# Two constants of a build-time planner: the pace of attention beside an MLP, and how late TensorE counts a cast of v

## The chip, the cores and the metric

The kernel runs on one core of a Trainium2 chip. The metric is device time in microseconds (us) of one execution. Thirteen runs of the kernel before gave a median of 348.4 us, from 345.13 to 350.83.

## What is computed

Attention with a causal mask, 8 batches and 8 heads, 576 query tokens, head size 64. Sixteen "beacon" keys and values stand ahead of the 576 own ones and are never masked. The attention output, as 4608 tokens by 512, goes through a two-layer MLP with a squared ReLU:

```python
k_all = np.concatenate([beacon_k, k], axis=2)
v_all = np.concatenate([beacon_v, v], axis=2)
scores = scale * np.matmul(q, k_all.transpose(0, 1, 3, 2))
scores = np.where(causal, -1e9, scores)
a = softmax(scores)
x = np.matmul(a, v_all)        # then (B, S, H*D) -> (4608, 512)
h = x @ w_in                   # 512 -> 2048
g = np.maximum(h, 0.0) ** 2
out = g @ w_out                # 2048 -> 512
```

## The kernel before

**Attention** works on pairs of heads: 4 pairs in each of 8 batches, pairs 0 to 31, so pair 16 is the first of batch 4, pair 20 of batch 5, pair 24 of batch 6, pair 28 of batch 7. From batch 1 on a pair has two groups of score matmuls (L622, into two PSUM strips each; the first group 4 matmuls, the second 8), four exponentials on ScalarE (L637), two causal minima on VectorE (L648, L651; "the mask"), and two attention-times-V groups of 15 matmuls, one per head (L674, into a PSUM tile `ps`). VectorE divides by the row sums (L692, L694) into `xn`. Groups of batch 0 are cut smaller.

**The MLP** works on chunks of 512 tokens, 9 chunks over 4608 tokens. A batch has 576 tokens, so chunk j crosses batches: chunk 3 needs batches 2 and 3, chunk 4 needs 3 and 4, chunk 5 needs 4 and 5. A chunk has 16 first-layer groups of 4 matmuls (L805; chunk 4 crosses the end of a ring buffer and has 8 of 256 columns, the first four of which need batch 3 alone; chunk 0 is cut into 240 and 272 columns), a ReLU each on ScalarE or VectorE (L821, L823), squares on VectorE (L830), and 16 second-layer groups of 4 matmuls (L840; "w_out groups"). ScalarE or VectorE copies the result to `osb` and SyncE stores it (L868).

**The MLP's input** is xT, the transpose of `xn`. For batches 0 to 2 TensorE transposes (L742); from batch 3 on SyncE issues five DMA transposes per batch (L725), of 112, 128, 128, 128 and 80 tokens. Chunk 3 needs the first three of batch 3, chunk 4 the first three of batch 4, chunk 5 the first two of batch 5.

**Loads.** q, k and v come in float32 pieces of up to 128 tokens (q0 to q4, k0 to k4, v0 to v4 of a batch) into eight staging buffers `stg` (L365; the beacons L364), on GpSimd's queue for batches 0 and 1, on SyncE's from batch 2 on. GpSimd casts each piece to bf16 (L320); the buffer is then free for another load. From batch 2 on SyncE issues two DMA transposes per batch (L398), qT after the five q casts and kT after the five k casts; scores need both. So SyncE's one queue, in program order, holds loads, the transposes of q and k, the transposes to xT, and the stores.

**What sets the order.** Nothing of the order is decided on the chip. `Order.run` (L69 to L190) plays the program through at build time: each operation has engines, a duration, a priority, dependencies and buffers, and each engine takes the ready operation of lowest priority number. The order in which it starts operations becomes the program's order on each engine; the chip keeps that order on each engine and waits on semaphores where data is late. Three things bear on the change:

- An operation that uses another's result is ready some time after it (L98 to L103). Users on TensorE have an event of their own, put off by the producer's `late`:

```python
heapq.heappush(events, (seen, seq, "done", op))
seq += 1
heapq.heappush(events, (seen + op.late, seq, "done_pe", op))
```

- Casts of v from batch 1 on have `late` 2.0 (L392). Their users on TensorE are the attention-times-V groups (L682 to L685).
- Attention is metered by MLP progress (L584, L591 to L594). `progress` sums the durations of the MLP groups started so far; pair p is held until it has reached

```python
return o.progress >= mlp_chunk_us * (LEAD + PACE * (p - HP))
```

with `mlp_chunk_us` 27.7, `LEAD` -0.4, `PACE` 0.255 and HP 4. MLP groups have priority numbers of 100,000 and more (L781), attention of some thousands at most, so attention runs as soon as its gate and its data allow, and the MLP fills the rest.

Of the kernel before, what the change touches and what calls it, by code (L numbers as in the profile page):

```python
# [45 lines left out]
class Order:  # L46
# [16 lines left out]
    def add(self, *a, **kw):  # L63
        op = Op(*a, **kw)
        op.need = [d for d in op.need if d is not None]
        self.ops.append(op)
        return op
# [126 lines left out]
def kernel(  # L194
# [116 lines left out]
    def rows_of(c):  # L311
        return 128 if c < NT - 1 else LAST
# [3 lines left out]
    def copy_on(e, dst, src):  # L316
        if e == "ACT":
            nc.scalar.copy(dst, src)  # L318
        else:
            eng[e].tensor_copy(dst, src)  # L320
# [12 lines left out]
    def t_start(t):  # L333
        return max(0, 128 * t - Nb)
# [14 lines left out]
    def add_load(b, x, c, prio, behind=[], sync=[]):  # L349
        t, beacon = src[x]  # L350
        lo = Nb if (c == 0 and beacon is not None) else 0
        if x == "q":
            t0, rows = 128 * c, min(128, S - 128 * c)
        else:
            t0, rows = t_start(c), rows_of(c)

        soft = b <= 1
        queue = nc.gpsimd if soft else nc.sync

        def emit_load(e):  # L360
            st = stg[ld.held[2]]
            insts = []
            if lo:
                insts.append(queue.dma_start(out=st[0:Nb], in_=beacon[b].transpose([1, 0, 2])))  # L364
            insts.append(queue.dma_start(out=st[lo:rows],  # L365
                                         in_=t[b, :, t0:t0 + rows - lo, :].transpose([1, 0, 2])))
            return insts

        ld = add(f"ld{b}{x}{c}", "POOL" if soft else "SP", 1.3 if lo else 0.65, emit_load,
                 prio=prio, take=("stg", "stg"), dma=(1.15 if b < NPE else 1.25) * rows / 128, behind=load_chain[-1:] + behind, sync=sync)  # L370
        load_chain.append(ld)

        def emit_cast(e):
            st = stg[ld.held[2]]
            if x == "v":
                copy_on(e, vb[b % 2][0:rows, c, :, 0:D], st[0:rows])
            else:
                dst = (qb if x == "q" else kb)[b % 2][0:rows, :, c, :]
                copy_on(e, dst, st[0:rows].rearrange("p (g u) d -> p g (u d)", u=2))

        deps = [ld]
        if x == "v" and b >= 2:
            deps += [o for p in range(HP * (b - 2), HP * (b - 1)) for o in av_ops[p]]
        if x != "v":
            if b < NPE + 2:
                deps += [zero_ops[b]]
            else:
                deps += trans[b - 2, x]
        engs = ("POOL", "DVE") if b == 0 and c <= 1 else ("POOL",)
        cast[b, x, c] = add(f"cast{b}{x}{c}", engs, {"DVE": 0.6, "POOL": 0.65}, emit_cast,  # L390
                            prio=prio if b else prio - 220.0, deps=deps, give=ld,
                            late=2.0 if x == "v" and b > 0 else 0.0)  # L392

    def add_trans(b, x, prio):
        srcb, dst = (qb, qT) if x == "q" else (kb, kT)
# [185 lines left out]
        return SPLIT if p < NSPLIT else WHOLE  # L581

    mlp_chunk_us = 27.7
    LEAD, PACE = -0.4, 0.255  # L584
    norm_ops = {}

    def add_pair(b, pr):
# [291 lines left out]
    late = []  # L879
    for b in range(B):  # L880
# [8 lines left out]
        for n, (x, c) in enumerate(([] if b < NPE else nat) + [("v", c) for c in range(NT)]):  # L889
            behind, sync = [], []  # L890
            if x == "v" and b == 0:
                pass
            elif x == "v" and b == 1 and c == 0:
                behind = [strided[1, 0, HP - 1, "q"]]
            elif b == 2 and n == 0:
                sync = [w_ops["out", 3]]
            elif b >= NPE and x == "v" and c == 0:
                for y in "qk":
                    add_trans(b, y, lp - 5.0)
                behind = trans[b, "q"] + trans[b, "k"]  # L900
            add_load(b, x, c, lp + 0.1 * n, behind, sync)
            if x == "v":
                v_loads[b].append(load_chain[-1])
# [13 lines left out]
        if b >= 1:  # L917
            for j in late:
                add_chunk(j)
            late = []  # L920
# [48 lines left out]
```

The softmax here doesn't subtract the row's maximum and nothing guards it: scores larger than these inputs give would overflow.

## Time and profile before

| what | value |
|---|---|
| median of 13 runs | 348.4 us |
| the profiled execution | 349.01 us |
| its span, first to last instruction of the program | 347.3 us |
| mean granted TensorE clock | 0.995 |
| TensorE's last matmul ends | 343.4 us |
| DMA traffic | 51.70 MB, mean 149 GB/s |

Times inside the span count from its first instruction; the 1.7 us between span and time lie around it. PE is TensorE's matmul stream, PEld its weight loads, DVE VectorE, ACT ScalarE, POOL GpSimd, SPq the queue of SyncE. "Busy" sums the time in which an instruction ran. In a wait line, the engine and line that waited come first, then what ended the wait, then total us, times and the longest. In a timeline line, start, length, engine, line, operation and operands; square brackets hold idle time ahead of it and what ended it. A DMA's length in SyncE's timeline is the time to issue it, not to land it; the view of a tile and the chain of waits give the landing. The trace misses 41 of 2957 matmul records, so a group of four can show as three.

### The profile page before, as it was taken

The numbers are of one execution on the slowest core, as the hardware profiler recorded it, in microseconds if no ns is written. First come the engines' busy times: TensorE is split into PE (matmuls) and PEld (weight loads), VectorE is DVE, ScalarE is ACT, GpSimd is POOL, SyncE is SP. The second block draws the span as 40 slices with busy tenths as digits, with TensorE's granted clock in tenths as the row PEclk, the third lists the DMA queues.
The fourth block names the chain that finished last, engine by engine and source line by source line (L and its number), as shares of the span: only waits on it lengthen the run. The fifth ranks groups of instructions, "written<-read, shape, count | busy, mean of one in ns | idle before, by whom it ended". The sixth has DMA issues, their size and how long they took to land.

```text
span 347.3 us, 7286 instructions
## 1 busy us (share of the span) xinstructions
PE 334.2 (96%) x2916; PEld 179.8 (52%) x2957; DVE 169.9 (49%) x366; ACT 193.8 (56%) x293; POOL 93.7 (27%) x144
## 2 busy tenths in 40 slices
PE   8999899999999999999989997999999999999995
PEld 7577665444554544445458743444444454444442
DVE  6796874258536852565336633473256412301300
ACT  3887664377657644775447644475467616615611
POOL 9674904325316425120523155012000000000000
PEclk9999999999999999999999999899999999999999
DMA  8999979999999999689999999891520032011002
GB/s 144 211 206 206 205 127 213 226 242 210 190 230 232 205 198 210 148 182 143 208 141 234 217 189 170 201 213 24 106 85 2 0 105 86 2 60 61 0 26 97
DMA packets 143664, 51.70 MB, mean 149 GB/s; under 512 B 130670, under 2 KB 138382, under 8 KB 143630
## 3 DMA queue, kind: packets, MB, share of 16 engines
q1 hardware_dynamic: 135231, 42.25, 61.8%
q0 software_dynamic: 7904, 8.69, 14.8%
q8 instruction: 23, 0.38, 0.5%
q10 hardware_dynamic: 495, 0.30, 0.3%
q14 instruction: 11, 0.09, 0.1%
HBM read 37.22 MB, written 9.44 MB: 134 GB/s over the span
## 4 chain that ended last, share of the span: by engine, by line
PE 75%; DMA 12%; POOL 5%; SPq 4%; issue 1%; DVE 1%; ACT 1%; POOLq 0%; ACTq 0%
PE ps L805 32%; PE ps L840 30%; PE strip L622 6%; PE ps L674 6%; DMA stg<-in_v_dram 4%; DMA qk_area<-in_q_dram 4%; DMA xT<-xn 3%; POOL qk_area L443 2%; DMA stg<-in_k_dram 1%; SPq L398 1%; SPq L725 1%; POOL vb L320 1%; SPq L365 1%; POOL stg L365 1%; PE ps L742 1%
## 5 line engine op out<-in xcount | busy, mean ns | idle before, releaser
L805 PE MATMUL ps<-xT,w_in 128*128 128x512 bf16 (+3 forms) x689 | 134.2, 342 | 4.2 <-DMA xT<-xn 3.5
L840 PE MATMUL ps<-w_out,g 128*128 128x512 bf16 x550 | 130.5, 379 | 1.8 <-issue 0.8
L637 ACT ACTIVATE pt<-strip 128x832 bf16<-128x832 f32 (+4 forms) x128 | 103.8, 863 | 28.6 <-PE strip L622 28.3
L805 PEld LDWEIGHTS <-w_in 128*128 128x128 bf16 x704 | 65.3, 98 | 60.6 <-issue 7.0
L821 ACT ACTIVATE g<-ps 128x512 bf16<-128x512 f32 (+2 forms) x123 | 68.4, 556 | 46.7 <-PE ps L805 45.8
L840 PEld LDWEIGHTS <-g 128*128 128x128 bf16 x576 | 52.5, 98 | 61.8 <-issue 4.4
L830 DVE TENSOR_TENSOR g<-g 128x1024 bf16<-128x1024 bf16 (+2 forms) x80 | 51.4, 647 | 58.6 <-ACT g L821 57.2
L320 POOL CAST qk_area<-stg 128x512 bf16<-128x512 f32 (+2 forms) x60 | 41.1, 692 | 59.8 <-DMA stg<-in_k_dram 39.2
L318 ACT COPY osb<-ps 128x512 f32<-128x512 f32 x32 | 18.8, 586 | 66.2 <-PE ps L840 45.6
L320 POOL CAST vb<-stg 128x512 bf16<-128x512 f32 (+1 forms) x39 | 26.5, 690 | 77.2 <-DMA stg<-in_v_dram 76.4
L674 PEld LDWEIGHTS <-pt 128*128 128x128 bf16 (+1 forms) x960 | 36.8, 98 | 14.0 <-issue 3.1
L674 PE MATMUL ps<-vb,pt 128*128 128x65 bf16 (+1 forms) x960 | 40.0, 194 | 1.3 <-POOL vb L320 0.9
L648 DVE TENSOR_TENSOR pt<-pt,tri 128x1024 bf16<-128x1024 bf16 (+1 forms) x36 | 24.5, 683 | 30.1 <-ACT pt L637 30.1
L622 PE MATMUL strip<-qT,kT 64*128 64x80 bf16 (+6 forms) x400 | 35.3, 279 | 0.0
L694 DVE TENSOR_TENSOR xn<-ps,rcp 128x320 bf16<-128x320 f32 (+2 forms) x64 | 31.5, 492 | 2.3
L692 DVE RECIPROCAL rcp<-ps 128x5 f32<-128x5 f32 (+2 forms) x64 | 12.3, 193 | 39.8 <-PE ps L674 39.4
L823 DVE TENSOR_SCALAR g<-ps 128x512 bf16<-128x512 f32 (+2 forms) x37 | 23.4, 632 | 17.1 <-PE ps L805 15.8
L622 PEld LDWEIGHTS <-kT 64*128 64x128 bf16 x400 | 12.0, 95 | 17.8 <-issue 14.0
L651 DVE TENSOR_TENSOR pt<-pt,tri 80x160 bf16<-80x160 bf16 x32 | 12.8, 398 | 0.0
L285 PE MATMUL ps<-g 128*128 128x256 bf16 (+1 forms) x71 | 10.9, 301 | 1.1 <-DVE warm L292 1.1
L365 POOL DMA_DIRECT2D stg<-in_v_dram x10 | 8.5, 852 | 5.2 <-DMA w_in<-in_moe_w_in_dram 3.9
L285 PEld LDWEIGHTS <-g 128*128 128x128 bf16 x71 | 6.8, 122 | 2.8 <-DVE warm L292 1.1
(41 smaller groups left out, 70.3 us busy)
## 6 DMA issues: line engine op xcount, KB each, us to landing
out_dram<-osb SPq DMA_DIRECT2D x17, 512.0 KB, 3.3
stg<-in_q_dram SPq DMA_DIRECT2D x24, 256.0 KB, 5.0
stg<-in_k_dram SPq DMA_DIRECT2D x18, 256.0 KB, 5.1
stg<-in_v_dram SPq DMA_DIRECT2D x18, 256.0 KB, 5.1
w_in<-in_moe_w_in_dram POOLq DMA_DIRECT2D x4, 512.0 KB, 9.2
w_out<-in_moe_w_out_dram POOLq DMA_DIRECT2D x4, 512.0 KB, 10.8
stg<-in_v_dram POOLq DMA_DIRECT2D x6, 256.0 KB, 8.5
stg<-in_k_dram SPq DMA_DIRECT2D x6, 224.0 KB, 3.8
```

The costliest lines, as they stand in the source:

```text
L318: nc.scalar.copy(dst, src)
L320: eng[e].tensor_copy(dst, src)
L622: nc.tensor.matmul(st[:, hj, at:at + t1 - t0], kT[b % 2][hp, pr, 128 * c:128 * c + 128], qT[b % 2][hp, pr, t0:t1], start=True, stop=True,)
L637: nc.scalar.activation(pt[take_pt.held[2]][:, :, off:off + width], st[:, :, 0:width], AF.Exp, bias=0.0, scale=scale)
L648: nc.vector.tensor_tensor(out=d, in0=d, in1=tri[:, m0:m0 + m, :][:, None].to_broadcast([128, 2, m, 128]), op=ALU.min)
L674: nc.tensor.matmul(a[:, at + (t - tl[0]) * (D + 1):at + (t - tl[0] + 1) * (D + 1)], P[0:rr, hj, o:o + 128], vb[b % 2][0:rr, c, 2 * pr + hj ...
L694: nc.vector.tensor_tensor(out=xn[b % 2].rearrange("p t (h d) -> p h t d", d=D)[:, h0:h0 + nh, tl[0]:tl[0] + nt], in0=a[:, :, :, 0:D], in1= ...
L805: nc.tensor.matmul(h[:, lo - spans[0][0]:hi - spans[0][0]], w_in_sb[:, mc, ft * 128:(ft + 1) * 128], xT[:, mc, lo % RING:lo % RING + hi - lo],
L821: nc.scalar.activation(dst, h, AF.Relu, bias=0.0, scale=1.0)
L823: nc.vector.tensor_scalar(out=dst, in0=h, scalar1=0.0, scalar2=None, op0=ALU.max)
L830: nc.vector.tensor_tensor(out=d, in0=d, in1=d, op=ALU.mult)
L840: nc.tensor.matmul(o, G[:, fc, ts * 128:(ts + 1) * 128], w_out_sb[:, fc, :], start=(fc == 0), stop=(fc == NFT - 1))
```

## The change

It alters two numbers that only the planner reads. `late` of the casts of v from batch 1 on goes from 2.0 to 5.0, so that the planner counts them as done for TensorE 5 us after they are, instead of 2. `PACE` goes from 0.255 to 0.245, so that pair p is let go at an MLP progress that is 0.277 us times (p - 4) smaller. No instruction is added or removed, and no operand, buffer count or dependency changes; the order of instructions on the engines, the choice between ScalarE and VectorE for some copies, and the buffer that each operation takes follow from the planner.

```diff
         cast[b, x, c] = add(f"cast{b}{x}{c}", engs, {"DVE": 0.6, "POOL": 0.65}, emit_cast,
                             prio=prio if b else prio - 220.0, deps=deps, give=ld,
-                            late=2.0 if x == "v" and b > 0 else 0.0)
+                            late=5.0 if x == "v" and b > 0 else 0.0)
...
     mlp_chunk_us = 27.7
-    LEAD, PACE = -0.4, 0.255
+    LEAD, PACE = -0.4, 0.245
```

## The prediction, made blind

> **What bounds the kernel now.** I read the busy times first, then TensorE's waits, then the stretches around the longest wait, then SyncE's queue there. The first line of the page, each engine's busy time with its share of the span:
>
> ```profile
> PE 334.2 (96%) x2916; PEld 179.8 (52%) x2957; DVE 169.9 (49%) x366; ACT 193.8 (56%) x293; POOL 93.7 (27%) x144
> ```
>
> TensorE (PE) is the bound. The change adds and removes no instruction on it, so it can only move the time through what TensorE waits for. Its waits: total us, times, longest.
>
> ```profile
> PE ps L805 <- DMA xT<-xn: 3.5, 3, 2.2
> ...
> PE ps L674 <- POOL vb L320: 0.9, 1, 0.9
> ```
>
> Three waits of the first MLP matmuls (L805) for the transposed attention output xT, and one of an attention-times-V matmul (L674) for a cast of v. The longest costs more than its 2.2 us. Stretches with us, busy time of PE, PEld, DVE, ACT, POOL, granted clock, DMA share, GB/s:
>
> ```profile
> 215.00:217.40 2.40, 0.20 (x2) 0.05 (x2) 0.69 (x1) 0.94 (x2) 0.61 (x1) 1.00 0.99 102
> 217.40:221.00 3.60, 3.60 (x16) 1.22 (x16) 0.69 (x1) 0.53 (x2) 0.00 (x0) 0.58 0.63 162
> ```
>
> After the idle the granted clock is 0.58. TensorE's own timeline there (start, length, what):
>
> ```profile
> 214.14 1.04 PE L840 MATMUL ps<-w_out,g 128*128 128x512 bf16 x4
> 217.38 3.05 PE L805 MATMUL ps<-xT,w_in 128*128 128x512 bf16 x8 [2.21 <-DMA xT<-xn]
> 220.37 0.77 PE L622 MATMUL strip<-qT,kT 64*128 64x336 bf16 x8
> ```
>
> Eight matmuls and the score group took until 221.06. At full clock four 512-column matmuls take 0.863 and this score group 0.41 (both from undisturbed stretches), so 2.14 instead of 3.68: 1.5 lost. The data could have been used from 214.14 + 0.86 = 215.0; so this place costs 2.4 + 1.5 = **3.8 us** (a little settles back later). The wait before it, at 178.4 for xT of batch 4, is 1.04, with the clock at 1.00 afterwards; the one at 140.9 is 0.25; the v wait at 40.7 is 0.93.
>
> Why was xT late? Its transposes (L725) stand in SyncE's queue, SyncE's timeline:
>
> ```profile
> 133.49 1.10 SPq L365 DMA_DIRECT2D stg<-in_k_dram  x1
> 134.68 1.09 SPq L365 DMA_DIRECT2D stg<-in_q_dram  x1
> 135.86 6.47 SPq L725 DMA_TRANSPOSE xT<-xn  x5
> 142.43 1.49 SPq L868 DMA_DIRECT2D out_dram<-osb  x1
> 144.04 3.95 SPq L398 DMA_TRANSPOSE qT<-qk_area  x1
> 148.08 0.54 SPq L868 DMA_DIRECT2D out_dram<-osb  x1
> 148.67 2.96 SPq L365 DMA_DIRECT2D stg<-in_k_dram  x3
> 156.39 4.23 SPq L398 DMA_TRANSPOSE kT<-qk_area  x1
> ...
> 208.27 3.12 SPq L365 DMA_DIRECT2D stg<-in_k_dram  x3
> 211.48 7.21 SPq L725 DMA_TRANSPOSE xT<-xn  x5
> ```
>
> The norms of batch 5 were not what xT waited for: TensorE did that batch's last attention-times-V group at 203.9. The five transposes waited for their turn behind loads until 211.48. Part of that delay is the hole from 151.6 to 156.4, in which SyncE waited for the last k piece to land and be cast before it could issue the kT transpose of batch 5.
>
> **Part 1: `late` 2.0 to 5.0.** It moves the first attention-times-V groups of batches 1 to 7 back. For batch 1 the built order puts five 0.44 first-layer groups and one 0.41 score group ahead of pair 4's group: it comes 2.6 later, at about 42.6, and the cast that it needs ended at 41.5. So 0.93 goes. What is late next: masks of pair 5 (VectorE has four squares, two relus and two norms ahead of them), 0.3 to 0.6; and then kT of batch 2. Its transpose was issued at 65.85 and landed 7.4 later, at 73.2 (the view of that tile); TensorE's first score group of batch 2 began at 73.43, with the same work ahead of it in both orders. SyncE's queue does not hang on TensorE there. TensorE, up to 0.9 earlier, waits for kT: I take a gain of **0.1** (bounds 0 and 0.3). Idle under 1.1 us left the clock at 1.00 in this trace.
>
> **Part 2: `PACE` 0.255 to 0.245.** Attention comes earlier. Counting groups in the two built orders, with 0.863 for a w_out group, 0.46 for attention-times-V, 0.51 and 0.41 for score groups: pair 16's scores come 3.9 earlier, pair 20's 4.3, pair 24's 5.2, pair 28's 7.4. First matmul of chunk 3: 0.45 earlier; of chunk 4: 1.3 earlier (two w_out groups fewer, a score group more ahead of it); of chunk 5: 1.84 later (two score groups, two attention-times-V groups more). GpSimd's order is the same. On SyncE, xT of batch 3 passes three loads of batch 5; all six remaining loads of that batch then run ahead of both its transposes; xT of batch 5 passes one load of batch 7, which comes after the qT transpose. Stores trade places with neighbours, 0.5 to 1.5 each.
>
> *SyncE's queue anew.* A store that moves ahead of a q piece of batch 4 can delay that batch's transposes by 0 to 0.9. xT of batch 3 starts at 132.5 to 133.4 instead of 135.86. Then 6.5 for it, 1.5 for the store, six loads from 140.5 to 141.4: the first lands 4.3 after issue (148.67 to 153.0 before), the others 1.2 apart. The third lands and is cast (1.0) by 148.2 to 149.1: qT, 3.95, a store, 0.54, and kT at 152.8 to 153.7, **2.7 to 3.6 earlier**; the last k piece is cast a microsecond before that, so the hole is gone. What follows moves by the same.
>
> - xT for chunk 3: lands 2.5 to 3.4 earlier, needed 0.45 earlier. The 0.25 goes: **0.2**.
> - xT for chunk 4: third piece landed at 179.33, now 175.7 to 176.6; needed at 178.4 - 1.3 = 177.1. **1.0** goes, by a margin of 0.5 to 1.4.
> - xT for chunk 5: starts at 206.3 to 207.8 (one load of 1.0 to 1.6 less as well); its second piece landed 5.77 after the first issue, so 212.1 to 213.6; needed at 215.0 + 1.84 - 1.0 = 215.8. **3.8** goes, by 2.2 or more.
>
> *What is nearest to being late then.* kT of batch 4 (landed 124.4, now up to 0.9 later; needed at 126.7): margin 1.4. v of batch 4: 2.0. kT of batch 5 (landed 162.6, now 159.0 to 159.9; needed at 162.1): 2.2. v of batch 5: 1.5. v of batch 7, behind the moved load (cast by 238.1 to 239.6, needed at 240.5): 0.9. Masks: second score group to attention-times-V takes 3.87 now and 3.6 at the tightest pairs after; scores to end of mask took 3.34 at 169.82. None is negative, but several are about 1 us, and a landing varies by 1 or 2 us (4.9 to 7.4 for kT). I charge **0.7** for what is late there (bounds 0 and 3).
>
> **Sum**, against the profiled execution's 349.0 (span 347.3): 349.0 - 0.1 - 0.2 - 1.0 - 3.8 + 0.7 = **344.6**. The median, 348.4, is 0.6 lower; I don't subtract that, since a faster run has probably less of the same waits.
>
> The Trainium skill, "TensorE: Matmul & The Clock Gate", Part 1 on the HAM clock gate, has the clock halved after an idle window of about 3.4 us. This trace has it at 0.58 after 2.2 us of idle. By the rule's length the slow clock would not belong to the wait, the chunk 5 term would be 2.4 and the time an estimated 346.1; I go by the row, since nothing else preceded the drop.
>
> **Rivals.**
> *The queue does not advance* (kT of batch 5 still at 156.4, the transfers being the limit: DMA share is 1.0 or more in most stretches up to 230). Then pair 20 waits 0.5, v 0.3, chunk 4 waits 1.5; chunk 5 still finds xT, since TensorE comes later and the transposes passed a load. Waits 2.3 in place of 4.8: 346.5. Against: SyncE's hole of 4.8 us at 151.6, in which nothing was issued.
> *New small waits take the gain*: the five margins near 1 us each go under by 0.5 to 1: 4 us back, 348. Or the waits of the profiled run are smaller in the median one.
> *Slower*: the three loads put behind five transposes hold kT of batch 5, pair 20 waits, and the clock drops. If the six loads land 2.2 apart (the slowest load issue here took 2.19) and not 1.2, and qT waits besides, kT comes 3 to 4 later than before: 3.5 to 4.5 of wait plus 1.5 for the clock, against 4.8 saved: 350.5 to 351. It decides from 3 us later than before, 6 later than I reckon.
> *Not what it says*: the built orders differ as described from the first attention-times-V group of batch 1, so this is out.
>
> **How the numbers follow.** Forecast (343 to 346) 0.62; queue not advancing 0.13; small waits 0.14; slower 0.11. About 0.5% (below 346.7, above 350.1) is what a measurement here can tell from no change. Faster: 0.62 and two thirds of 0.13, 0.71; slower 0.11; the rest, 0.18, the same. Range 342.6 (all margins hold, 343.9, less part of the 0.6) to 348.6, leaving out the slower case and the edges of the others.
>
> **What would show it.** Right: no wait of L805 for xT at chunk 5, clock 1.00 around 217, kT of batch 5 issued near 153, xT of batch 5 near 207; a new wait of L622 for kT near 72.5. Wrong: SyncE's queue not earlier at 153, waits for kT or v at pairs 16, 20 or 28, a granted clock below 1.00 anywhere past the start.

## The result and the profile after

The changed kernel's median is 343.36 us (11 runs, 342.31 to 344.77; a twelfth took 344.78), against 347.52 for the kernel before (48 runs, 344.39 to 350.83): ratio 0.9889 [0.9863, 0.9915]. Measured again later beside other runs of before it came to 0.9891 [0.985, 0.9933]. The forecast was 344.6 with a range of 342.6 to 348.6; the profiled execution took 343.28, 5.7 less than the one of before (spans 347.3 and 341.6). Ratios here and below, and counts of runs by their clock, leave out runs more than 1.5% above the fastest of their kernel.

From the page of the kernel after, the busy times and the line of the chain that ended last, by engine:

```profile
PE 332.5 (97%) x2919; PEld 179.3 (52%) x2957; DVE 172.5 (51%) x373; ACT 189.7 (56%) x286; POOL 92.4 (27%) x144
...
PE 92%; DMA 3%; SPq 1%; issue 1%; ACT 0%; DVE 0%; ACTq 0%
```

The same line of the chain on the page of the kernel before:

```profile
PE 75%; DMA 12%; POOL 5%; SPq 4%; issue 1%; DVE 1%; ACT 1%; POOLq 0%; ACTq 0%
```

TensorE's work is what it was (its busy time fell by 1.7, about the 1.5 that the slow clock cost at chunk 5). What left the chain are DMA, POOL and SPq, 21% of a span before and 4% after: loads, casts and SyncE's queue. TensorE's waits after (total, times, longest):

```profile
PE ps L285 <- DVE warm L292: 1.1, 1, 1.1
PE ps L805 <- DMA xT<-xn: 1.0, 2, 0.6
PE ps L478 <- ACT g L821: 0.5, 1, 0.5
```

The three waits for xT, 3.5 us, are two of 1.0 together, and the wait of L674 for a cast of v is gone. The wait that cost most was at chunk 5. The same two stretches as in the prediction (us, busy PE, PEld, DVE, ACT, POOL, granted clock, DMA share, GB/s), and TensorE's timeline there:

```profile
215.00:217.40 2.40, 2.35 (x13) 1.00 (x11) 1.43 (x4) 1.88 (x3) 0.00 (x0) 1.00 0.74 137
217.40:221.00 3.60, 3.60 (x24) 1.54 (x23) 2.64 (x5) 2.49 (x4) 0.00 (x0) 1.00 1.04 256
```

```profile
214.77 0.58 PE L622 MATMUL strip<-qT,kT 64*128 64x496 bf16 x4
215.28 2.76 PE L805 MATMUL ps<-xT,w_in 128*128 128x512 bf16 x11
217.98 0.48 PE L622 MATMUL strip<-qT,kT 64*128 64x336 bf16 x8
```

Chunk 5's first matmuls (L805) start at 215.28 right behind a score group, without a bracket for a wait; the clock stays at 1.00, and 24 matmuls run where 16 ran before. The two waits that are left:

```profile
139.63 1.02 PE L805 MATMUL ps<-xT,w_in 128*128 128x512 bf16 x4 [0.61 <-DMA xT<-xn]
...
176.49 0.60 PE L805 MATMUL ps<-xT,w_in 128*128 128x256 bf16 x4 [0.43 <-DMA xT<-xn]
```

SyncE's timeline after, where the cause was sought:

```profile
133.81 7.01 SPq L725 DMA_TRANSPOSE xT<-xn  x5
140.93 1.15 SPq L868 DMA_DIRECT2D out_dram<-osb  x1
142.18 0.41 SPq L365 DMA_DIRECT2D stg<-in_q_dram  x1
142.68 1.19 SPq L365 DMA_DIRECT2D stg<-in_k_dram  x1
143.96 1.19 SPq L365 DMA_DIRECT2D stg<-in_q_dram  x1
145.25 2.78 SPq L365 DMA_DIRECT2D stg<-in_k_dram  x3
149.27 3.23 SPq L398 DMA_TRANSPOSE qT<-qk_area  x1
152.59 0.53 SPq L868 DMA_DIRECT2D out_dram<-osb  x1
153.21 4.56 SPq L398 DMA_TRANSPOSE kT<-qk_area  x1
...
204.85 1.64 SPq L365 DMA_DIRECT2D stg<-in_k_dram  x2
206.58 8.00 SPq L725 DMA_TRANSPOSE xT<-xn  x5
```

All six loads of batch 5 that were left stand ahead of its qT transpose, and kT is issued at 153.21, where before three of them stood behind qT and kT had to wait until 156.39. The queue then runs about 3 us earlier, one load of batch 7 fewer stands ahead of xT of batch 5, and that starts at 206.58, before at 211.48. That load, the last k piece of batch 7, now stands behind its own qT (218.55), and kT of batch 7 follows only at 223.01: the hole is back one step later, where it costs nothing, since that kT landed at 228.30 and was asked for at 232.2. No run puts the hole of batch 5 back by itself; that closing it made the advance is read from the two timelines.

**Where the 5.7 us came from.** How much earlier TensorE starts the same group, less the groups that the new order puts ahead of it or takes away, is its lead (in most rows the start is that of the group's weight load). The last column is the lead less the one of the row above.

| TensorE starts | before | after | from the order | lead | gained here |
|---|---|---|---|---|---|
| first 240-column group of chunk 0 | 37.26 | 36.32 | 0 | 0.9 | 0.9 |
| scores of batch 2 | 73.43 | 71.66 | 0 | 1.8 | 0.8 |
| first matmul of chunk 3 | 141.10 | 139.59 | -0.45 | 1.1 | -0.7 |
| scores of pair 20 | 166.61 | 161.13 | -4.31 | 1.2 | 0.1 |
| scores of pair 24 | 204.66 | 197.71 | -5.18 | 1.8 | 0.6 |
| third group of chunk 5 | 221.06 | 216.81 | +1.43 | 5.7 | 3.9 |
| last group | 342.13 | 336.41 | 0 | 5.7 | 0 |

Chunk 5 is 3.9 of the 5.7. The first 0.9 is not the change's: up to that group TensorE's order is the same in both kernels, and it starts anywhere from 36.3 to 37.3 in five profiles (37.26 before, 36.72 and 37.22 in the two of E1 below, 36.32 and 36.53 in the two of the changed kernel). From there to batch 2 it gained 0.8, about the 0.93 of the v wait that is gone. Chunk 3 took 0.7 back, and about as much came again by pair 24.

### The profile page after: what moved, and what is told of

Read it like the earlier page. It is cut to its first block, busy times and chain, and to the rows that moved or that the text cites. A ratio compares the mean times of both kernels' runs of the same rounds, so it can differ in the third digit from the quotient of the medians.

```text
span 341.6 us, 7282 instructions
## 1 busy us (share of the span) xinstructions
PE 332.5 (97%) x2919; PEld 179.3 (52%) x2957; DVE 172.5 (51%) x373; ACT 189.7 (56%) x286; POOL 92.4 (27%) x144
## 3 DMA queue, kind: packets, MB, share of 16 engines
HBM read 37.22 MB, written 9.44 MB: 137 GB/s over the span
## 4 chain that ended last, share of the span: by engine, by line
PE 92%; DMA 3%; SPq 1%; issue 1%; ACT 0%; DVE 0%; ACTq 0%
PE ps L805 35%; PE ps L840 34%; PE ps L674 9%; PE strip L622 9%; PE ps L285 3%; DMA kT<-qk_area 2%; DMA xT<-xn 1%; PE ps L478 1%; SPq L725 1%; PE ps L742 1%; ACT g L821 0%; PE ps L475 0%; ACT osb L318 0%; DVE xn L694 0%; SPq L868 0%
## 5 line engine op out<-in xcount | busy, mean ns | idle before, releaser
L805 PE MATMUL ps<-xT,w_in 128*128 128x512 bf16 (+3 forms) x691 | 132.5, 340 | 1.8 <-DMA xT<-xn 1.0
L805 PEld LDWEIGHTS <-w_in 128*128 128x128 bf16 x704 | 65.4, 98 | 57.0 <-issue 5.7
L821 ACT ACTIVATE g<-ps 128x512 bf16<-128x512 f32 (+2 forms) x120 | 66.6, 555 | 45.1 <-PE ps L805 42.6
L840 PEld LDWEIGHTS <-g 128*128 128x128 bf16 x576 | 52.9, 98 | 60.6 <-issue 2.4
L320 POOL CAST qk_area<-stg 128x512 bf16<-128x512 f32 (+2 forms) x60 | 39.4, 661 | 66.0 <-DMA stg<-in_k_dram 36.1
L318 ACT COPY osb<-ps 128x512 f32<-128x512 f32 x27 | 15.8, 586 | 56.9 <-PE ps L840 51.9
L674 PEld LDWEIGHTS <-pt 128*128 128x128 bf16 (+1 forms) x960 | 36.2, 98 | 14.0 <-issue 3.5
L674 PE MATMUL ps<-vb,pt 128*128 128x65 bf16 (+1 forms) x960 | 39.8, 194 | 0.1
L622 PE MATMUL strip<-qT,kT 64*128 64x80 bf16 (+6 forms) x400 | 35.0, 277 | 0.3
L823 DVE TENSOR_SCALAR g<-ps 128x512 bf16<-128x512 f32 (+2 forms) x40 | 25.0, 634 | 13.6 <-PE ps L805 12.6
L622 PEld LDWEIGHTS <-kT 64*128 64x128 bf16 x400 | 12.0, 94 | 17.9 <-issue 13.5
L320 DVE COPY osb<-ps 128x512 f32<-128x512 f32 x9 | 6.2, 692 | 17.7 <-PE ps L840 17.3
L651 DVE TENSOR_TENSOR pt<-pt,tri 80x160 bf16<-80x160 bf16 x32 | 11.2, 351 | 0.0
```

The source lines that it names most:

```text
L622: nc.tensor.matmul(st[:, hj, at:at + t1 - t0], kT[b % 2][hp, pr, 128 * c:128 * c + 128], qT[b % 2][hp, pr, t0:t1], start=True, stop=True,)
L674: nc.tensor.matmul(a[:, at + (t - tl[0]) * (D + 1):at + (t - tl[0] + 1) * (D + 1)], P[0:rr, hj, o:o + 128], vb[b % 2][0:rr, c, 2 * pr + hj ...
L805: nc.tensor.matmul(h[:, lo - spans[0][0]:hi - spans[0][0]], w_in_sb[:, mc, ft * 128:(ft + 1) * 128], xT[:, mc, lo % RING:lo % RING + hi - lo],
L821: nc.scalar.activation(dst, h, AF.Relu, bias=0.0, scale=1.0)
L823: nc.vector.tensor_scalar(out=dst, in0=h, scalar1=0.0, scalar2=None, op0=ALU.max)
L840: nc.tensor.matmul(o, G[:, fc, ts * 128:(ts + 1) * 128], w_out_sb[:, fc, :], start=(fc == 0), stop=(fc == NFT - 1))
```

## The experiments

Theory: the gain comes from SyncE's queue. The pace moves the transposes to xT ahead of loads, and the loads of a batch together ahead of its qT transpose, so that xT of batch 5 lands before TensorE asks for it. Rivals: the gain comes from the casts of v (`late`); or it is the slow clock after the wait, more than the wait; or the changed order on TensorE itself makes it. Ratios are against the kernel before, run beside the experiment.

### E1, the pace alone

```diff
-    LEAD, PACE = -0.4, 0.255
+    LEAD, PACE = -0.4, 0.245
```

> PACE 0.245 alone, late left at 2.0. From pair 16 on its TensorE order has the same counts ahead of each group as the changed kernel, and SyncE's queue is the same but for three stores. Theory (the queue advances by some 3 us because the last loads of batch 5 run in one piece): kT of batch 5 issued near 153, xT of batch 5 near 207, no wait at chunk 5, a time within 0.5 us of the changed kernel (343.4), the 0.9 us wait for v of batch 1 back but taken out of the wait for kT of batch 2. Rival (late is needed for the gain): the wait for v returns and adds to the time, 344.3 or more.

Measured: 344.53, ratio 0.9898 [0.984, 0.9955]. TensorE's longest waits:

```profile
PE ps L674 <- POOL vb L320: 2.7, 5, 0.9
...
PE strip L622 <- DMA kT<-qk_area: 0.6, 1, 0.6
```

No wait for xT is left at all (xT of batch 5 starts at 208.68, chunk 5 needs it at 218.60), in exchange for five small waits for casts of v. TensorE reaches chunk 3 at 143.53, after the changed kernel's 139.63, and as I read it that is why it finds xT there. These runs missed my numbers: kT of batch 5 was issued at 155.68, not near 153, and 344.53 is on the rival's side of 344.3, in six runs that go from 342.46 to 346.60.

The same kernel again:

> PACE 0.245 alone, beside the changed kernel. Theory now (late moves the groups that use v past the casts, which in the first run of this kernel were waited for five times, 2.7 us in all; late also moves the store behind v1): v waits of 0.5 to 2.7 in the profile, 0.5 to 1.5 us slower than the changed kernel. Rival (the waits come out of later ones): the same within 0.4.

343.95, ratio 0.988 [0.9843, 0.9916], beside 344.25 for the changed kernel run next to it, with one v wait of 0.9 for POOL. I had expected it 0.5 to 1.5 slower than the changed kernel; it is 0.3 faster, within the rival's 0.4. The pace alone carries the gain, as far as these runs can tell. Over both sets of runs the pace alone has 344.02 (12 runs) and both constants 343.58 (18): what `late` adds can't be told from nothing.

### E2, `late` alone

```diff
-                            late=2.0 if x == "v" and b > 0 else 0.0)
+                            late=5.0 if x == "v" and b > 0 else 0.0)
```

> late 5.0 alone, PACE left at 0.255. TensorE's order from pair 16 on is that of the kernel before; SyncE's queue still changes: xT of batch 3 passes one load, the loads of batch 5 run ahead of both its transposes, and xT of batch 4 comes behind three more loads. Theory (the place in SyncE's queue decides): kT of batch 5 near 152.5 instead of 156.4, xT of batch 4 near 172, wait at chunk 4 between 0.3 and 1.0, xT of batch 5 near 207.6, no wait at chunk 5; 2.5 to 4 us faster than before. Rival (attention has to come earlier for xT to be in time, which is PACE): chunk 5 still waits about 2 us with a slow clock after it, and the time is that of before within 1 us.

Measured: 349.04, ratio 1.0019 [0.9978, 1.006]: nothing gained, as the rival had it. I had expected its xT of batch 5 to start at 207.6; it started at 211.62. That part of my reading was wrong. TensorE's timeline at chunk 5:

```profile
218.27 3.23 PE L805 MATMUL ps<-xT,w_in 128*128 128x512 bf16 x8 [3.08 <-DMA xT<-xn]
```

SyncE's timeline of this kernel in the next batch says why:

```profile
181.55 3.87 SPq L398 DMA_TRANSPOSE qT<-qk_area  x1
185.53 0.52 SPq L868 DMA_DIRECT2D out_dram<-osb  x1
186.10 0.47 SPq L365 DMA_DIRECT2D stg<-in_k_dram  x1
191.18 3.01 SPq L398 DMA_TRANSPOSE kT<-qk_area  x1
...
208.36 3.17 SPq L365 DMA_DIRECT2D stg<-in_k_dram  x3
211.62 7.46 SPq L725 DMA_TRANSPOSE xT<-xn  x5
```

kT of batch 5 was indeed 2.2 earlier (154.20), but xT of batch 4, behind three more loads, started at 172.68, as before (172.70), and now a k load of batch 6 stands behind that batch's qT, and the same hole opens there, from 186.6 to 191.2. And xT of batch 5 still follows three loads. So an earlier queue in batch 5 is not enough: the hole must not come back, and the loads must not stand ahead of xT.

The same kernel again:

> late 5.0 alone once more, beside the same kernel with filling matmuls. Theory and rival both expect 349.0 within 0.6; the profile shows whether the wait at chunk 5 and the slow clock after it come back.

348.75, ratio 0.9991 [0.9957, 1.0026], waits for xT of 5.8 in its profile. It confirms the first.

### E3, three loads behind xT, the rest as before

The order of the kernel before, with the last three k loads of batch 7 and their casts put behind xT of batch 5. TensorE's order is that of before.

```diff
+        moved = ("ld7k2", "ld7k3", "ld7k4", "cast7k2", "cast7k3", "cast7k4")
+        held = [x for x in issued if x[0].name in moved]
+        issued = [x for x in issued if x[0].name not in moved]
+        at = [x[0].name for x in issued].index("xt5.4") + 1
+        issued[at:at] = held
```

> The kernel before, with only the loads k2, k3, k4 of batch 7 and their casts put behind the five xT transposes of batch 5; TensorE's order is untouched. Theory (at chunk 5 xT is late through what stands ahead of it in SyncE's queue): the transposes start near 208.3 instead of 211.5, the second piece lands near 214, no wait at chunk 5, no clock drop, 3.0 to 3.8 us faster than before. Rival (the transfers, not the queue, are the limit): xT lands at 216 or later, the wait shrinks by under 1 us.

Measured: 345.16, ratio 0.9922 [0.9896, 0.9947]. Lines of this kernel stand five further on (L730 is L725, L810 is L805). SyncE's timeline, then TensorE's:

```profile
208.31 7.29 SPq L730 DMA_TRANSPOSE xT<-xn  x5
215.70 2.09 SPq L370 DMA_DIRECT2D stg<-in_k_dram  x3
```

```profile
214.88 1.04 PE L845 MATMUL ps<-w_out,g 128*128 128x512 bf16 x4
215.76 1.89 PE L810 MATMUL ps<-xT,w_in 128*128 128x512 bf16 x8
```

xT starts 3.2 earlier, chunk 5 begins right behind the w_out group, and its eight matmuls take 1.89 where they took 3.05. This is 2.7 of the 4.2 us between the medians, without one instruction moved on TensorE. The rival that the order on TensorE makes the gain falls for this part. I had expected 3.0 to 3.8. Of the 27 runs of before beside it, 18 have no low clock (a mean granted clock above 0.996), with a median of 347.34: against these E3 is 2.2 faster. So the wait itself is most of this gain, and the rival that it is more the slow clock falls with it.

### E4 and E7, the wait without the slow clock

18 matmuls of 256 columns ahead of chunk 5's first group, from weights that have long been loaded, into the PSUM tile that the group then overwrites. They put about 2 us of work in the place of the wait (L804; the first layer's line becomes L808).

```diff
+                        for _ in range(18 if (j, ft) == (5, 0) else 0):
+                            nc.tensor.matmul(h[:, 0:256], w_in_sb[:, 0, 0:128], w_in_sb[:, 0, 0:256],
+                                             start=True, stop=True)
```

E4 is the kernel before with this edit:

> The kernel before, with 18 matmuls of 256 columns (0.107 us each, 1.9 in all) that write what the first group of chunk 5 then overwrites, ahead of that group: they stand in TensorE's 2.2 us of idle. Theory (the idle itself drops the clock, at a price of 1.4): the granted clock stays at 1.00 from 217 to 221 and the time falls by 1.0 to 1.5 us, though 18 matmuls are added. Rival (the clock fell for another reason, or the idle is all of the price): no change, or up to 1.9 slower in executions in which xT is not late.

Measured: 347.61, ratio 0.999 [0.996, 1.002]. TensorE's timeline and the stretch of 217.4 to 221:

```profile
215.03 2.13 PE L804 MATMUL ps<-w_in 128*128 128x256 bf16 x18
216.99 1.89 PE L808 MATMUL ps<-xT,w_in 128*128 128x512 bf16 x8
```

```profile
217.40:221.00 3.60, 3.60 (x24) 1.57 (x23) 2.09 (x4) 1.90 (x3) 0.00 (x0) 1.00 0.84 219
```

The clock is 1.00, and in none of the 12 runs was the mean granted clock of the execution at 0.996 or less (in 9 of 27 runs of before beside it). Yet the median didn't move. The 1.0 to 1.5 that the theory gave is not there, and the runs of before say why: 18 of those 27 had no low clock, so their median hardly contains it, and E4's 347.61 is near the 347.34 of these 18. The means are 347.88 before and 347.40 here; a price of 1.4 in 9 of 27 runs would make 0.5, but 0.5 is also within the noise (0.7).

E7 is the same edit on E2's kernel, whose wait is longer:

> late 5.0 alone, with the 18 filling matmuls (1.9 us) ahead of the first group of chunk 5. With late alone 11 of 12 executions showed a mean granted clock of 0.995 or less, against 11 of 29 of the kernel before, so this is where the slow clock can be priced. Theory (idle drops the clock, the price is about 1.4): mean granted clock 0.998 or more in nearly all executions and a median 1.0 to 1.6 us below that of late alone in this call. Rival (the slow clock costs nothing, since TensorE would wait later anyway): the same time as late alone.

Measured: 348.35, ratio 1.0 [0.9971, 1.003], 0.4 below `late` alone run next to it, not the 1.0 to 1.6 expected. In the two profiles the time from chunk 5's first group to its third was 2.24 with the filling and 3.34 without, so 1.1 is there locally. Low clocks (0.996 or less) fell from 10 of 11 runs to 3 of 12, and the means differ by 0.1, with an interval of 1.1 to either side: a price of 1 us in most runs is neither shown nor excluded. That the clock has a price after the wait is shown in single executions; its share in the time here stays open.

### E5, the places in the queue that still wait

The changed kernel, with one load of batch 5 put behind xT of batch 3, and two of batch 6 behind xT of batch 4.

```diff
+        for names, last in ((('ld5q2', 'cast5q2'), 'xt3.4'),
+                            (('ld6q3', 'ld6k1', 'cast6q3', 'cast6k1'), 'xt4.4'),):
+            held = [x for x in issued if x[0].name in names]
+            issued = [x for x in issued if x[0].name not in names]
+            at = [x[0].name for x in issued].index(last) + 1
+            issued[at:at] = held
```

> The changed kernel, with xT of batch 3 put ahead of one more load on SyncE (q2 of batch 5) and xT of batch 4 ahead of two more (q3, k1 of batch 6); TensorE's order untouched. Theory (the two waits left, 0.61 at chunk 3 and 0.43 at chunk 4, are places in SyncE's queue too, and nothing else is late behind them): both waits go, xT of batch 4 starts near 167.4 instead of 169.6, 0.6 to 1.0 us faster than the changed kernel, about 342.5. Rival (the loads put behind come late in their turn): kT of batch 5 or 6 lands later and TensorE waits there, the time is that of the changed kernel or more.

Measured: 343.57, ratio 0.9854 [0.9817, 0.9892]. Its profile has a span of 340.9 and, after the start, two short waits:

```profile
PE strip L627 <- DMA kT<-qk_area: 0.6, 2, 0.4
```

Both waits for xT are gone (xT of batch 4 starts at 167.88 instead of 169.56). Again, with the changed kernel run next to it:

> The changed kernel with xT of batches 3 and 4 further ahead on SyncE, beside the changed kernel itself. Theory: no wait for xT, 0.4 to 1.0 us faster than the changed kernel in this call. Rival: the same within 0.3, the earlier ratio of 0.9854 being chance.

342.84 (342.31 to 343.31), ratio 0.9846 [0.9811, 0.988], 1.4 below the changed kernel beside it, more than the 0.4 to 1.0 expected. Over both sets of runs it is 343.06 (12 runs) against 343.58 (18). It is the best version here, by 0.5 to 1.4 us; its profiled span is 0.7 shorter.

### E6, a store put back ahead of a load

In the changed kernel kT of batch 2 lands 6.64 after its issue, before 7.36. The first store of chunk 0 had moved behind a load of v there. E6 puts it back.

```diff
+        for names, last in ((('ld2v1',), 'st0.3'),):
+            held = [x for x in issued if x[0].name in names]
+            issued = [x for x in issued if x[0].name not in names]
+            at = [x[0].name for x in issued].index(last) + 1
+            issued[at:at] = held
```

> The changed kernel, with one store of chunk 0 put back ahead of piece v1 of batch 2 on SyncE, as before the change. In six profiles with the store behind v1, kT of batch 2 landed 6.2 to 6.9 us after its issue; in four with it ahead, 7.0 to 7.6. Theory (the store's 512 KB share the transfer engines with that transpose): 7.0 or more again, the first scores of batch 2 0.5 to 0.8 later, and the end unchanged within 0.4, because TensorE then waits less for xT at chunks 3 and 4. Rival (chance, or v1 itself): 6.2 to 6.9 as in the changed kernel.

Measured: kT of batch 2 landed 6.29 after issue, in one profile. That is not the 7.0 or more that the store would have made; my theory fell. The time, 344.72, ratio 0.9917 [0.9883, 0.9951], is 0.5 above the changed kernel beside it; the intervals overlap.

The changed kernel itself, run beside E6:

> The changed kernel once more, beside the others of this call. Both theories expect a ratio of 0.989 within 0.003, waits of 0.2 to 1.0 at chunks 3 and 4, none at chunk 5.

344.25, ratio 0.9891 [0.985, 0.9933]; two waits for xT, 0.9 together, and one of L622 for kT of batch 2 at 72.06, 0.3.

### E8, the pace a step further

```diff
-    LEAD, PACE = -0.4, 0.245
+    LEAD, PACE = -0.4, 0.235
```

> The changed kernel with PACE 0.235: attention earlier still. SyncE's queue puts xT of batch 4 and of batch 5 ahead of four more loads each, but the scores of pair 20 come 3.5 us earlier than in the changed kernel (161.1 to about 157), and kT of batch 5, whose place in the queue is the same, landed at 159.3. Theory (what bounds the step is kT): TensorE waits 1.5 to 2.5 for kT of batch 5, with the clock slow after it at times, no wait at chunks 3 to 5, 345 to 346.5. Rival (the earlier attention, the better, since xT is what is late): 343.4 or less.

Measured: 346.29, ratio 0.9928 [0.9894, 0.9961]: by the ratios about a third of the gain is lost. TensorE's timeline at pair 20, and the stretch behind it:

```profile
160.56 0.76 PE L622 MATMUL strip<-qT,kT 64*128 64x496 bf16 x4 [2.36 <-DMA kT<-qk_area]
```

```profile
160.00:165.00 5.00, 4.44 (x15) 1.56 (x16) 1.38 (x2) 2.18 (x3) 1.10 (x2) 0.66 1.02 200
```

No wait for xT remains, but kT of batch 5, issued at 153.32 and landed at 160.52, is now 2.4 late, mostly because pair 20 asks earlier (at 158.20; the changed kernel at 161.13), in part because it took 7.2 to land (6.1 there), and the granted clock drops to 0.66. This is the wait that the rival "slower" of the prediction named, one step beyond the change and from the other side: there kT came late, here above all pair 20 asks early.

## Why the prediction held, point by point

- **What bounds it.** TensorE's waits, the one for xT at chunk 5 ahead of all. Right: E3 gives 2.7 us by that place alone. What the sum took for it, though, was one execution with a low clock, 1.5 slower than the median of 48 runs.
- **Part 1, `late`: 0.1 expected.** The v wait of batch 1 went, as said. That kT of batch 2 would take the gain back was wrong in the profiled execution: I held its landing fixed at 73.2, and it landed at 71.62, partly by an earlier issue (65.0 for 65.8), partly by a faster landing. TensorE was 1.8 ahead there, 0.9 of it from a start-up that the change doesn't touch, and chunk 3 took 0.7 of the 1.8 back. In the medians `late` shows nothing (E1 against both constants, and E2). In five executions with the casts at 2.0 (E1, E3, E4 and before) kT of batch 2 landed 7.0 to 7.6 after issue, in nine with 5.0 it was 6.1 to 6.9. Why is open; it isn't the store (E6).
- **Part 2, SyncE's queue.** kT of batch 5 was expected at 152.8 to 153.7 and issued at 153.21; xT of batch 5 at 206.3 to 207.8, started at 206.58; its second piece at 212.1 to 213.6, landed at 212.96; the third piece for chunk 4 at 175.7 to 176.6, landed at 176.35. xT of batch 3 started at 133.81, 0.4 after the latest that I gave.
- **Chunk 3 (0.2) and chunk 4 (1.0).** Mis-sized: TensorE lost 0.7 of its lead at chunk 3 and won 0.6 by chunk 4. Chunk 4's landing was as reckoned; chunk 3's third piece landed at 139.49, 1.5 earlier than before's 141.00 and not 2.5 to 3.4. What failed most is the need: I took TensorE to be 0.1 ahead of before, and it came 1.8 earlier, so it stood 0.61 and 0.43 for transposes that would otherwise have been in time. E5 removes exactly these by moving three loads.
- **Chunk 5 (3.8).** It gave 3.9 in the profiled executions. In E3's medians the place is worth 2.7, and 2.2 against runs without the low clock. The 1.5 for the clock was right for the profiled execution and is missing in most: 28 of 72 runs of before show a low clock. The lead was held to the end without loss.
- **New small waits (charged 0.7).** None past the two of the table: the margins at kT of batch 4, 5 and 7 and v of batch 7 all held (kT of batch 5 landed at 159.34, pair 20 asked at 161.13; kT of batch 7 at 228.30, asked at 232.2). So the 4.4 expected became 5.7 in the profiled pair: 0.7 for this charge and 1.7 more at part 1 (0.9 of it the start-up), less 0.9 at chunk 3 and 0.4 at chunk 4, and 0.2 of small differences. The medians differ by 4.2. That this is so near to the 4.4 of the sum is partly luck: the terms err in both directions, and the sum starts from an execution with the low clock.
- **The rivals.** "The queue does not advance" is out by the timeline. "Slower by kT of batch 5" did not decide here, but at `PACE` 0.235 a wait for that kT does. Of "the waits of the profiled run are smaller in the median one" a part is true, by the clock.
- **The clock.** I set the row above the rule of the Trainium skill, "TensorE: Matmul & The Clock Gate", Part 1 on the HAM clock gate. That the drop belongs to the wait held: it came again after 2.36 of idle in E8 and 3.08 in E2. But the length does not decide alone: idle of 2.59 (E7, at 142.1) and of 2.28 (E2's second profile, at 142.6), both ahead of chunk 3, left the clock at 1.00. What decides is worked out from the traces in the last section. The page says besides that the window is free-running. These traces agree with that, and with its length of about 3.4 us; they differ in that 2.2 us of idle within a window were enough.
- **Slips of the working.** 2.4 + 1.5 is 3.9, not 3.8. With 2.4 for chunk 5 the sum is 346.0, not 346.1. The rival "slower" by its own terms gives 349.2 to 350.2, not 350.5 to 351. The slowest load issue on SyncE before took 2.96 (a v piece at 197.46), not 2.19. None of them moves the forecast by more than 0.1.

## What to carry to other kernels

Where one engine's queue issues loads, transposes and stores in program order, read when its critical transfer is issued and not only when its input is ready: xT of batch 5 waited for its turn, and three loads put behind it were worth 2.7 us with nothing else touched. Look for a load that stands behind a wait of its own group, as the last k loads behind qT: it opens a hole for the whole queue, and an order that closes it in one batch can open it in the next (E2). A pacing constant has an edge on both sides (at 0.255 the MLP waited for xT, at 0.235 attention for kT), and a lead that an early step wins counts only up to the next landing that it doesn't move. Before a term is taken from one profile, see whether most runs have what it prices: here the mean granted clock of each run told that most had no slow clock.

## What the runs showed of the hardware

- **The granted clock changes on a fixed grid.** The four profiles with a drop in mid-run (before, both of E2, E8) have exactly one stretch at 0.50 each, 3.413 us long. The stretches at 1.00 before and after it last whole multiples of that: 62 and 37 in before and in the first of E2, 63 and 37 in the second, 46 and 53 in E8. So in these traces the clock changes only at multiples of 3.41 us from its first rise, wherever the kernel's waits lie. The stretches that matter, cut along that grid, first in the kernel before, then in E2's second profile (us, busy PE, PEld, DVE, ACT, POOL, granted clock, DMA share, GB/s):

```profile
214.54:217.95 3.41, 1.21 (x6) 0.42 (x5) 0.69 (x1) 1.41 (x2) 0.85 (x2) 1.00 0.90 104
217.95:221.36 3.41, 3.41 (x16) 1.08 (x14) 0.95 (x2) 0.89 (x2) 0.00 (x0) 0.50 0.60 173
```

```profile
138.19:141.61 3.42, 2.13 (x24) 0.92 (x22) 0.77 (x3) 2.42 (x3) 1.84 (x3) 1.00 0.82 165
141.61:145.02 3.41, 2.42 (x17) 1.07 (x18) 0.69 (x1) 0.49 (x2) 0.00 (x0) 1.00 0.41 83
```

- In the kernel before, the whole wait of 2.21 lies in one such window, and the clock halves when the window ends, half a microsecond after TensorE has resumed. In E2's second profile a wait of 2.28 is cut by a boundary into 1.29 and 1.00, and nothing happens. E7's 2.59 is cut into 1.26 and 1.33. Over the fourteen profiles, from 36 to 330 us, every window with 2.2 us or more of idle (2.21, 2.36, 2.43, 2.46) was followed by a halved clock, and none with 1.4 or less. No window between these was seen. So a wait of one length can cost the clock in one execution and not in the next.
- One halved window costs at most 1.7 us (half of 3.41, an estimate), and it lowers the mean granted clock over 347 us by 0.005, to the 0.995 of the profiled run. Over 72 runs of the kernel before, 28 had a mean of 0.996 or less; their median is 349.34, that of the other 44 is 347.28. The changed kernel had it in 2 of 18 runs, E1, E3 and E5 in none of 12 each. The 2.1 us between the two groups are more than one window can cost; whether longer waits make the rest isn't separated.
- One DMA transpose of k for a whole batch took 6.1 to 7.6 us from issue to landing in batch 2, over fourteen profiles, and 7.2 in batch 5 of E8, where the changed kernel had 6.1. In batch 2, two profiles of one kernel differed by up to 0.5. A margin of 0.5 us at such a transfer can be gone in the next execution, and one of 1.5 us in another order.
- In SyncE's timeline the hole is not a slow instruction. The k load of 0.47 at 186.10 in E2 is followed by nothing for 4.6 us; the piece's cast ends at 191.15, and kT is issued at 191.18. The Trainium skill, "DMA: Bandwidth & Descriptors", section on the anatomy of one DMA (for DMAs that GpSimd issues), says that a semaphore is waited for on the issuing sequencer, ahead of the dispatch. This hole on SyncE agrees with that, and everything behind the waiting transpose waits with it.
